# One issue order for every engine, read from a table: attention and two gated layers on one core

## The chip, the cores and the metric

The kernel runs on 1 core of one Trainium2 chip. The core has five engines with an instruction queue each: TensorE (PE in the profile, its weight loads PEld), VectorE (DVE), ScalarE (ACT), GpSimd (POOL) and SyncE (SP), which here issues every transfer. The metric is the device time of one execution in microseconds (us); less is better.

## The reference

A linear attention with 4 batches, 8 heads, 576 positions and a head width of 64 is followed by two gated layers over 2304 tokens (512 to 1536 to 512); all of it is float32.

```python
def phi(x):
    proj = np.einsum('bhsd,df->bhsf', x, w_phi)
    proj = proj - np.max(np.abs(proj), axis=-1, keepdims=True)
    return np.concatenate([np.exp(proj), np.exp(-proj)], axis=-1)
q_p, k_p = (phi(q), phi(k))
kv = np.einsum('bhsf,bhsd->bhfd', k_p, v)
z = np.sum(k_p, axis=2)
num = np.einsum('bhsf,bhfd->bhsd', q_p, kv)
den = np.einsum('bhsf,bhf->bhs', q_p, z)[..., None] + 1e-06
x = num / den
...
g = x @ w_gate
x = silu(g) * (x @ w_val) @ w_out
...
gate = 1.0 / (1.0 + np.exp(-(x @ w_gate)))
return gate * (x @ w_val) @ w_out
```

## The kernel before

**Attention** goes in 41 steps of 128 positions of 4 heads; the keys run 5 steps ahead of the queries. In a step, `proj` (L354) multiplies keys and queries by w_phi into one pair of PSUM banks, `a`, of which there is only one. `shift` on DVE takes the largest magnitude (L368, tile `m`) and subtracts it (L370, tile `sub`); only then may the next `proj` write `a`. `exps` on ACT (L377, tile `ek`) exponentiates the keys, `k_sum` (L397) adds them up against the values, `turn` (L419) transposes the queries, `turn_exp` on ACT (L430, tile `eq`) exponentiates these, and `ratio` (L447, bank `d`) makes numerators and denominators, which `ratio_out` (L453, tile `nd`) copies out on ACT. `den_load`, `den_inv` (L473 and L474 on DVE, tile `rc`) and `den_store` fetch denominators from DRAM, invert them and store them.

**Weights** arrive as float64 and are turned into float32 in 72 rounds (`plan_round`): `load` (tile `raw`), `mag` (L173) and `tail` (L176) on ACT, three `lead` operations on DVE (L181 to L187, tile `wcv`), `add` (L194) on POOL or DVE and mostly a `store` to DRAM. 18 rounds lie beside the attention. `plan_slot` and `plan_x_block` then form sums of quarters of weights and activations and split each into a high part (L223, on ACT) and a low part (L218, on DVE), so that a float32 product is three matmuls.

**The layers** (two of them, each in two halves of the width 1536) go over blocks of 512 or 256 tokens and pairs of width chunks. `product` (L664, banks `a` and `b`) makes seven products of quarters instead of eight; `keep` (L684) copies a bank to SBUF on ACT while later products go on adding into the same bank, `add` (L690) adds on DVE, `gate` (L702, ACT) and `gated` (L707, DVE) follow, their result is split (L714, L715) and `accumulate` (L736, L738, banks `c` and `d`) multiplies it by the output weights. For the first layer, `load_num` fetches numerators (tile `xraw`) and inverted denominators (tile `rb`), and `norm` (L584) multiplies them.

**The order.** Every step is registered with a time (`Plan.at`), worked out from a few constants (`STEP`, `RL`, `W2` and others), and the steps are traced in the order of these times. The framework's scheduler then puts the instructions of each engine in an order of its own, from a cost model: it may move an instruction ahead of an earlier one that it thinks is not ready, and it may part the instructions of one step. `issue_after` holds some copies and multiplications (in `mag`, `halves`, `norm`) behind the last instruction noted in `anchor`. On the chip each engine works through its own list in that order and waits at an instruction whose inputs are not there.

Of the kernel before, what the change touches and what calls it, by code (L numbers as in the profile page):

```python
# [2 lines left out]

# [6 lines left out]
F32 = mybir.dt.float32  # L10
# [79 lines left out]


class Plan:

# [17 lines left out]
def body(ctx: ExitStack, tc: tile.TileContext, qT, kT, v, w_phi2, wpk, out):  # L111
# [40 lines left out]

    anchor = {"early": True}
    stored = set()

    def plan_round(t, l, p, i, home=None):
# [62 lines left out]

    def halves(hi, lo, src, act):  # L220
        act = act or anchor["early"]
        with tc.issue_after(anchor["act" if act else "dve"].ins):
            (nc.scalar.copy if act else nc.vector.tensor_copy)(hi, src)  # L223
        low(hi, lo, src)

    def plan_slot(t, hh, p, gap=3.0, out=14.0):
# [30 lines left out]
        def split(w, m):  # L257
            if (hh, p) not in wts:
                wts[hh, p] = [pools[f"w{p}"].tile([P, 2, 2, 7, P], R32, tag=f"w{p}{x}",
                                                  name=f"w{p}{x}{hh}") for x in "hl"]  # L260
            d, src = ((slice(0, 4), a), (slice(4, 7), s))[m]
            halves(*(x[:, w, :, d] for x in wts[hh, p]), src[w], WA)

# [7 lines left out]
        def split_out():  # L271
            hi, lo = wts[hh, p, "o"]
            halves(hi, lo, lo.bitcast(F32), WA)

        def split_home():
            wts[hh, p, "o"] = [pools[f"w{p}"].tile([P, 2, DM], R32, tag=f"o{p}{x}",
                                                   name=f"o{p}{x}{hh}") for x in "hl"]
            halves(*wts[hh, p, "o"], a[2], WA)

        if not isinstance(t, float):  # L280
            for i, u in enumerate(t):
                e = plan_round(u, l, q, i, home)
                if i < 4 and i % 2:
                    at(e + 0.8, sums, i // 2)
                    for m in range(2):
                        at(e + 2.4 + 1.5 * m, split, i // 2, m)
                elif i == 5:
                    at(e + 1.0, split_home)
# [8 lines left out]
        at(t + out + 4.0, split_out)  # L297


    def plan_attention(ap, ak, ae, aq, t0):  # L300
# [4 lines left out]
        def consts():  # L305
            nc.sync.dma_start(out=w2, in_=w_phi2)
            make_identity(nc, ident)

        at(-99.0, consts)

        n = 2 * NT
# [45 lines left out]
        def shift(r, kinds):  # L357
# [6 lines left out]
            else:  # L364
# [4 lines left out]
                                    apply_absolute_value=True)  # L369
            anchor["dve"] = nc.vector.tensor_tensor(  # L370
                out=y, in0=x, in1=mm.to_broadcast(list(x.shape)), op=ALU.subtract)

        def exps(r):
            r["e"] = ak.tile([P, 4, 2, F], F32, tag="ek", name="ek", bufs=EB)
            e = r["e"].rearrange("p (c i) s f -> p i c s f", i=2)
            for s in range(2):
                anchor["act"] = nc.scalar.activation(e[:, :, :, s], r["sub"][:, :, 1], AF.Exp,  # L377
                                                     scale=-1.0 if s else 1.0)
# [44 lines left out]
        def turn_exp(i, c):  # L423

            qd, tt = divmod(i, NT)
            for g, lo, hi in here(tt):
                if (qd, g) not in eqt:
                    eqt[qd, g] = aq.tile([P, 4, 2, 320], F32, tag="eq", name="eq", bufs=EB)
                d = slice(lo - GROUPS[g][0], hi - GROUPS[g][0])
                anchor["act"] = nc.scalar.activation(  # L430
                    eqt[qd, g][:, :, c, d], qt[i]["pt"][:, :, lo - tt * P:hi - tt * P], AF.Exp,
                    scale=-1.0 if c else 1.0)
# [125 lines left out]
    def plan_x_block(t, hh, j, gap):  # L558
        n = BLOCKS[j][1]
        full = n == 2 * NQ  # L560
        t0 = BLOCKS[j][0]
        b, s, rb = {}, {}, {}

# [17 lines left out]
        def norm(c, k):  # L581
            x = b[c][:, k, :n]
            with tc.issue_after(anchor["dve"].ins):
                nc.vector.tensor_tensor(out=x, in0=x, in1=rb[c][:, k, :n], op=ALU.mult)  # L584

        def keep_x(c):

            if j not in ROUTE[1][:2]:
                nc.sync.dma_start(out=xo[0][j][:, c], in_=b[c][:, :, :n])
                stored.add(("x", 0, j, c))  # L590
            b[c] = b[c].rearrange("p k n -> p (k n)")[:, :2 * n] if full else b[c][:, :, :n]
            b[c] = b[c].rearrange("p (q n) -> p q n", n=NQ) if full else b[c]

# [6 lines left out]
        def sums(c):  # L600
# [4 lines left out]
            if full:  # L605
                b11, b12, b21, b22 = (b[c][:, k] for k in range(4))
                t3, t2, t4 = (s[c][:, k] for k in range(3))
# [4 lines left out]
                tt(out=t4, in0=b21, in1=t2, op=ALU.subtract)  # L612
                rb[c] = t1
            else:
                tt(out=s[c][:, 0], in0=b[c][:, 1], in1=b[c][:, 0], op=ALU.subtract)

        def split(c, m):
# [4 lines left out]
            if full:  # L622
                src, d = ((b[c][:, 0], 0), (rb[c], 1), (b[c][:, 2:4], slice(2, 4)),
                          (s[c][:, :2], slice(4, 6)), (s[c][:, 2], 6))[m]
            else:
                src, d = ((b[c], slice(0, 4, 2)), (s[c][:, 0], 4))[m]
            halves(*(x[:, c, d] for x in xs[hh, j]), src, XA)

# [8 lines left out]
        for c in range(2):  # L637
# [3 lines left out]
            for k in range(m):  # L641
                at(t + 5.0 + gap * (2 * c + 2 * k / m), split, c, k)

# [36 lines left out]
    def keep(r, k):  # L680


        src, d = {1: ("x", 0), 5: ("y", 3), 6: ("x", 1)}[k]
        anchor["act"] = nc.scalar.copy(part_of(r, d), parts(r, src))  # L684

    def add(r, d):


        c = part_of(r, d)
        anchor["dve"] = nc.vector.tensor_tensor(out=c, in0=parts(r, "zy x"[d]), in1=c, op=ALU.add)  # L690

# [17 lines left out]
    def gated_split(r, j, f):  # L709
        n = BLOCKS[j][1]  # L710
        v = r["c", f][:, 1].rearrange("p t n -> p (t n)")[:, :n]
        hi, lo = (pools["u"].tile([P, 2 * NQ], R32, tag=f"u{x}{f}", name=f"u{x}{f}")[:, :n]
                  for x in "hl")
        nc.scalar.copy(hi, v)  # L714
        nc.vector.tensor_tensor(out=lo, in0=v, in1=hi, op=ALU.subtract)  # L715
        r["u", f] = hi, lo

# [91 lines left out]
    def plan_unit(t, r, hh, j, p, last):  # L809
# [4 lines left out]
        for k in ORDER_LAST if (hh, j, p) == (3, len(BLOCKS) - 1, NPAIR - 1) else ORDER[full]:  # L814
# [14 lines left out]
            for d in ([3] if full and k == 7 else [2] if k == 4 else  # L829
# [3 lines left out]
                if d != 3:  # L833
                    at(e + 1.2, gated_split, r, j, d // 2)
        return t
# [19 lines left out]

    at(T0, lambda: anchor.update(early=False))
    T0 += TS
# [19 lines left out]
    SG, XG = 2.72, 2.13  # L877
    XA, WA, OA = True, True, 2

# [62 lines left out]
```

## Time and profile before

| | |
|---|---|
| median of 3 runs | 1056.11 us (1052.02 to 1059.38) |
| profiled execution | 1062.7 us, its span 1060.7 us, granted TensorE clock 0.994 |
| PE | 1021.9 us busy, 96% of the span; weight loads 905.9 us, 85% |
| DVE, ACT, POOL | 690.8, 534.5 and 24.0 us busy |
| chain that ended last, by engine | PE 61%, transfers 13%, DVE 10%, ACT 4% |

The span runs from the first to the last instruction of the program; 2.0 us of the execution lie around it. Busy times overlap, so they don't add up to the span. A matmul's recorded time is longer than the distance to the next matmul's start, since they are pipelined.

### The profile page before, as it was taken

The numbers are of one execution on the slowest core, as the hardware profiler recorded it, in microseconds if no ns is written. First come the engines' busy times: TensorE is split into PE (matmuls) and PEld (weight loads), VectorE is DVE, ScalarE is ACT, GpSimd is POOL, SyncE is SP. The second block draws the span as 40 slices with busy tenths as digits, with TensorE's granted clock in tenths as the row PEclk, the third lists the DMA queues.
The fourth block names the chain that finished last, engine by engine and source line by source line (L and its number), as shares of the span: only waits on it lengthen the run. The fifth ranks groups of instructions, "written<-read, shape, count | busy, mean of one in ns | idle before, by whom it ended". The sixth has DMA issues, their size and how long they took to land.

```text
span 1060.7 us, 20675 instructions
## 1 busy us (share of the span) xinstructions
PE 1021.9 (96%) x8488; PEld 905.9 (85%) x8488; DVE 690.8 (65%) x1246; ACT 534.5 (50%) x1029; POOL 24.0 (2%) x24
## 2 busy tenths in 40 slices
PE   6798999999999999999999999999999999999998
PEld 5565666688899899999899988999889999999997
DVE  4787775576785877546868698567586752463533
ACT  4667775654554555436445455455455542332422
POOL 0111110000000000000000000000000000000000
PEclk9899999999999999999999999999999999999999
DMA  5545655532664553106646444064344100331111
GB/s 184 160 151 169 201 179 155 176 104 95 194 214 131 169 169 100 40 24 206 189 142 207 137 153 159 20 206 165 127 140 159 60 21 18 122 120 40 41 40 40
DMA packets 67838, 135.99 MB, mean 128 GB/s; under 512 B 9696, under 2 KB 36000, under 8 KB 67744
## 3 DMA queue, kind: packets, MB, share of 16 engines
q1 hardware_dynamic: 67744, 134.68, 40.4%
q8 instruction: 66, 1.08, 0.4%
q14 instruction: 28, 0.23, 0.1%
HBM read 94.66 MB, written 39.99 MB: 127 GB/s over the span
## 4 chain that ended last, share of the span: by engine, by line
PE 61%; DMA 13%; DVE 10%; ACT 4%; issue 2%; SPq 1%; POOL 0%; DVEq 0%; ACTq 0%
PE a L664 20%; PE b L664 14%; DMA raw<-wpk 6%; PE c L738 6%; PE d L738 5%; PE d L736 4%; PE c L736 4%; PE d L447 3%; DMA xo<-o 2%; PE a L354 2%; DVE c L690 1%; DMA b<-xo 1%; PE c L397 1%; PE b L419 1%; DMA part<-o 1%
## 5 line engine op out<-in xcount | busy, mean ns | idle before, releaser
L702 ACT ACTIVATE c<-c 128x256 f32<-128x256 f32 x96 | 50.3, 524 | 146.8 <-DVE c L690 146.8
L684 ACT COPY c<-a 128x512 f32<-128x512 f32 x96 | 56.1, 585 | 103.0 <-PE a L664 92.6
L715 DVE TENSOR_TENSOR ul<-c,uh 128x512 fp32r<-128x512 f32 (+1 forms) x120 | 75.8, 636 | 46.7 <-ACT uh L714 46.3
L714 ACT CAST uh<-c 128x512 fp32r<-128x512 f32 (+1 forms) x120 | 68.8, 577 | 62.3 <-DVE c L707 57.1
L690 DVE TENSOR_TENSOR c<-b,c 128x512 f32<-128x512 f32 x96 | 65.7, 685 | 46.7 <-PE b L664 44.6
L664 PE MATMUL a<-xh,w1h 128*128 128x256 f32 x288 | 80.8, 280 | 2.0 <-DVE c L690 1.1
L664 PE MATMUL a<-xh,w2h 128*128 128x256 f32 x288 | 80.6, 280 | 1.8 <-ACT c L684 1.8
L664 PE MATMUL a<-xh,w0h 128*128 128x256 f32 x288 | 80.8, 281 | 1.5 <-DVE c L690 1.5
L181 DVE TENSOR_SCALAR wcv<-wcv 128x512 f32<-128x512 f32 x72 | 31.1, 431 | 78.4 <-ACT wcv L173 78.1
L664 PE MATMUL a<-xl,w0h 128*128 128x256 f32 x288 | 80.4, 279 | 0.0
L664 PE MATMUL a<-xl,w2h 128*128 128x256 f32 x288 | 80.4, 279 | 0.0
L664 PE MATMUL a<-xh,w0l 128*128 128x256 f32 x288 | 80.4, 279 | 0.0
L664 PE MATMUL a<-xh,w2l 128*128 128x256 f32 x288 | 80.4, 279 | 0.0
L664 PE MATMUL a<-xl,w1h 128*128 128x256 f32 x288 | 80.3, 279 | 0.0
L664 PE MATMUL a<-xh,w1l 128*128 128x256 f32 x288 | 80.3, 279 | 0.0
L176 ACT ACTIVATE raw<-raw 128x512 int32<-128x512 uint32 x72 | 48.7, 677 | 53.3 <-DMA raw<-wpk 52.6
L447 PE MATMUL d<-eq,z 128*32 128x320 f32 (+3 forms) x512 | 69.6, 422 | 4.9 <-ACT nd L453 3.0
L707 DVE TENSOR_TENSOR c<-c 128x256 f32<-128x256 f32 x96 | 53.3, 556 | 25.6 <-ACT c L702 25.2
L354 PEld LDWEIGHTS a<-w,x 64*128 64x128 f32 x576 | 39.0, 199 | 31.8 <-issue 19.6
L368 DVE TENSOR_REDUCE m<-a 128x8 f32<-128x1024 f32 (+1 forms) x41 | 44.7, 1091 | 31.1 <-PE a L354 30.7
L354 PE MATMUL a<-w,x 64*128 64x128 f32 x576 | 47.8, 301 | 17.5 <-DVE sub L370 9.6
L664 PE MATMUL b<-xh,w2h 128*128 128x256 f32 x224 | 62.5, 279 | 0.7 <-ACT c L684 0.7
(179 smaller groups left out, 3176.1 us busy)
## 6 DMA issues: line engine op xcount, KB each, us to landing
raw<-wpk SPq DMA_DIRECT2D x72, 512.0 KB
wf<-wcv SPq DMA_DIRECT2D x40, 256.0 KB
a<-wf SPq DMA_DIRECT2D x20, 512.0 KB
b<-xo SPq DMA_DIRECT2D x16, 512.0 KB
part<-o SPq DMA_DIRECT2D x13, 512.0 KB
o<-part SPq DMA_DIRECT2D x13, 512.0 KB
wfo<-wcv SPq DMA_DIRECT2D x20, 256.0 KB
v<-v SPq DMA_DIRECT2D x36, 132.0 KB
```

The costliest lines, as they stand in the source:

```text
L176: nc.scalar.activation(r["lo"].bitcast(I32), r["lo"], AF.Copy, scale=2.0 ** -29)
L354: nc.tensor.matmul(r["ps"][:, i, n, c], xt[kind, qd, j][d, c, o:o + P], w2[d], start=True, stop=True)
L447: nc.tensor.matmul(pn[i * w:(i + 1) * w, :m], f, e[:, h, c, :m], start=(c == 0), stop=(c == 1))
L664: nc.tensor.matmul(o, f[:, c], x[:, c], start=k == first and w == 0 and c == 0 and m == 0, stop=c == 1 and m == 2, skip_group_check=True)
L684: anchor["act"] = nc.scalar.copy(part_of(r, d), parts(r, src))
L690: anchor["dve"] = nc.vector.tensor_tensor(out=c, in0=parts(r, "zy x"[d]), in1=c, op=ALU.add)
L702: nc.scalar.activation(o, g, AF.Silu if hh < 2 else AF.Sigmoid)
L707: nc.vector.tensor_tensor(out=o, in0=v, in1=places(r, j, 0, d)[1], op=ALU.mult)
L714: nc.scalar.copy(hi, v)
L715: nc.vector.tensor_tensor(out=lo, in0=v, in1=hi, op=ALU.subtract)
L736: nc.tensor.matmul(ps[:, :n], a[:, k], x, start=st, stop=sp)
L738: nc.tensor.matmul(ps, x[:, k], a, start=st, stop=sp)
```

## The change

A table `TIMES` gives an issue time for each of the 3586 steps, in hundredths of a us, by the name of the step's function; `Plan.at` takes the next one of that name and leaves the time worked out from the constants unused. The steps are traced in the order of these times under `tc.manual_schedule()`, so that each engine's list is that order: no scheduler moves anything, and the instructions of one step stay together. `issue_after` and `anchor` go. So that the table can place the high and the low part of a split apart, `halves` becomes two steps, `high` and `rest`. Work, tiles, buffers and engines are the same, instruction by instruction.

```diff
+TIMES = {
...
+    "proj": (
...
 class Plan:
     def __init__(self):
         self.events = []
+        self.given = {name: iter(times) for name, times in TIMES.items()}
     def at(self, t, fn, *args):
+        if self.given:
+            t = next(self.given[fn.__name__])
         self.events.append((t, len(self.events), fn, args))
...
         def mag():
             r["w"] = scratch("wcv", U32)[:, :HW]
-            with tc.issue_after(anchor["act"].ins):
-                nc.scalar.activation(r["w"].bitcast(F32), r["hi"].bitcast(F32), AF.Abs)
+            nc.scalar.activation(r["w"].bitcast(F32), r["hi"].bitcast(F32), AF.Abs)
...
-    def halves(hi, lo, src, act):
-        act = act or anchor["early"]
-        with tc.issue_after(anchor["act" if act else "dve"].ins):
-            (nc.scalar.copy if act else nc.vector.tensor_copy)(hi, src)
-        low(hi, lo, src)
+    def plan_halves(t, views):
+
+        def high():
+            hi, _, src = views()
+            nc.scalar.copy(hi, src)
+
+        def rest():
+            low(*views())
+
+        at(t, high)
+        at(t + 0.6, rest)
...
-                at(t + 6.0 + gap * (2 * w + m), split, w, m)
+                plan_halves(t + 6.0 + gap * (2 * w + m), partial(split, w, m))
...
-    plan.issue()
+    with tc.manual_schedule():
+        plan.issue()
```

The order that comes of it, at three places. **Place A** is on ACT in the attention, around the step whose keys are exponentiated at 83.9 us of the profiled execution; `ek<-sub` is the exponential of the keys, `eq<-b` that of the queries, `nd<-d` the copy of a ratio, `w1h` the high part of a weight, and the rows that read `raw` are `mag` and `tail` of a round. Before:

```order
L377 ACTIVATE ek<-sub 128x2x2x128 x2
L173 ACTIVATE wcv<-raw 128x512
L176 ACTIVATE raw<-raw 128x512
L430 ACTIVATE eq<-b 128x4x128
L223 CAST w1h_1151<-a 128x2x512
L430 ACTIVATE eq<-b 128x4x128
L453 COPY nd<-d 128x256 x2
L377 ACTIVATE ek<-sub 128x2x2x128 x2
```

In the changed kernel, from the same exponential on:

```order
L722 ACTIVATE ek<-sub 128x2x2x128 x2
L798 COPY nd<-d 128x256
L562 CAST w1h_1130<-a 128x2x512
L775 ACTIVATE eq<-b 128x4x128 x2
L562 CAST w1h_1130<-s 128x2x384
L722 ACTIVATE ek<-sub 128x2x2x128 x2
L798 COPY nd<-d 128x256
L511 ACTIVATE wcv<-raw 128x512
```

The copy `nd<-d` moves ahead of the cast and of the queries, and the next row of the kind `raw<-raw` (L514) comes only nine rows after the last of these, behind two more exponentials of keys.

**Place B** is on DVE, near the end of the attention; `rc` is a tile of denominators that a transfer brings. Before:

```order
L368 TENSOR_REDUCE m<-a_2300 128x8
L473 TENSOR_SCALAR rc<-rc 128x18
L370 TENSOR_TENSOR sub<-a_2300,m 128x1024
L474 RECIPROCAL rc<-rc 128x18
L368 TENSOR_REDUCE m<-a_2361 128x4
L370 TENSOR_TENSOR sub<-a_2361,m 128x2x256
```

In the changed kernel, at the same step:

```order
L928 TENSOR_TENSOR xraw<-xraw,rb 128x512 x4
L713 TENSOR_REDUCE m<-a_2325 128x8
L715 TENSOR_TENSOR sub<-a_2325,m 128x1024
L556 TENSOR_TENSOR xl<-xraw,xh 128x256
L713 TENSOR_REDUCE m<-a_2387 128x4
L715 TENSOR_TENSOR sub<-a_2387,m 128x2x256
L556 TENSOR_TENSOR xl<-xraw,xh 128x256
L957 TENSOR_TENSOR t<-xraw 128x256
L958 TENSOR_TENSOR rb<-xraw 128x256
L959 TENSOR_TENSOR t<-xraw,rb 128x256
L960 TENSOR_TENSOR t<-xraw,t 128x256
L818 TENSOR_SCALAR rc<-rc 128x18
```

The denominators no longer part a reduction from its subtraction and come after two steps' worth of both; the four multiplications of `norm` for the first block, which stood behind this step, stand ahead of it.

**Place C** is on ACT in the first layer, in the fourth block of the route; `c<-a` and `c<-b` are `keep`, `xh` is the high part of the next block's activations. Before:

```order
L684 COPY c_4371<-b 128x2x256
L223 CAST xh<-xraw 128x256
L176 ACTIVATE raw<-raw 128x512
L173 ACTIVATE wcv<-raw 128x512
L223 CAST xh<-rb 128x256
L223 CAST xh<-xraw 128x512
L223 CAST xh<-t 128x512
L223 CAST xh<-t 128x256
L684 COPY c_4349<-a 128x2x256
```

In the changed kernel, from the same first row on:

```order
L1034 COPY c_4350<-b 128x2x256
L562 CAST xh<-t 128x256
L1034 COPY c_4321<-a 128x2x256
L562 CAST xh<-xraw 128x256
L514 ACTIVATE raw<-raw 128x512
L562 CAST xh<-xraw 128x512
L511 ACTIVATE wcv<-raw 128x512
L514 ACTIVATE raw<-raw 128x512
```

The `keep` of the unit's product 6 stood behind seven rows of preparation and now stands behind one.

## Rows read from the trace of the kernel before

**Rows 1.** The page's busy times: busy us, share of the span, instructions of each engine.

```profile
PE 1021.9 (96%) x8488; PEld 905.9 (85%) x8488; DVE 690.8 (65%) x1246; ACT 534.5 (50%) x1029; POOL 24.0 (2%) x24
```

**Rows 2.** Busy time by stretch (start:end in us, length, engines, clock, DMA share, GB/s).

```profile
20.90:67.20 46.30, 39.78 (x578) 28.80 (x578) 38.46 (x49) 31.78 (x63) 7.75 (x6) 0.93 0.51 149
67.20:139.50 72.30, 66.67 (x941) 44.14 (x940) 55.36 (x73) 51.78 (x105) 11.62 (x9) 0.98 0.61 185
139.50:175.70 36.20, 35.68 (x553) 25.15 (x552) 24.04 (x27) 23.88 (x52) 3.89 (x3) 1.00 0.64 176
175.70:201.80 26.10, 23.33 (x242) 14.14 (x242) 19.18 (x39) 16.05 (x39) 0.00 (x0) 0.93 0.46 147
201.80:1057.00 855.20, 843.45 (x6011) 782.79 (x6009) 545.82 (x1048) 402.63 (x762) 0.00 (x0) 1.00 0.37 118
```

**Rows 3.** The same stretches for L354 alone (`proj`): PE busy (x), PEld busy (x).

```profile
20.90:67.20 46.30, 11.38 (x144) 9.70 (x144) 0.93 0.51 149
67.20:139.50 72.30, 15.70 (x208) 12.94 (x208) 0.98 0.61 185
139.50:175.70 36.20, 9.56 (x128) 7.90 (x128) 1.00 0.64 176
```

**Rows 4.** Waits from 67.2 to 139.5 us: us in total, times, longest us.

```profile
ACT raw L176 <- DMA raw<-wpk: 10.1, 7, 2.6
DVE wcv L181 <- ACT wcv L173: 9.9, 7, 2.3
...
PE d L447 <- ACT nd L453: 3.0, 2, 1.8
```

**Rows 5.** Timeline from 83 us: start, length, instruction, [idle before <- releaser].

```profile
85.61 0.43 DVE L181 TENSOR_SCALAR wcv<-wcv 128x512 f32<-128x512 f32 x1 [2.11 <-ACT wcv L173]
...
87.60 0.68 ACT L176 ACTIVATE raw<-raw 128x512 int32<-128x512 uint32 x1 [2.02 <-DMA raw<-wpk]
...
90.08 0.64 ACT L453 COPY nd<-d 128x256 f32<-128x256 f32 x2
...
90.50 0.62 PE L447 MATMUL d<-eq,z 128*32 128x256 f32 x2 [1.75 <-ACT nd L453]
```

**Rows 6.** Timeline of DVE from 175 us.

```profile
176.98 1.23 DVE L368 TENSOR_REDUCE m<-a 128x8 f32<-128x1024 f32 x1 [1.64 <-PE a L354]
181.18 0.18 DVE L473 TENSOR_SCALAR rc<-rc 128x18 f32<-128x18 f32 x1 [2.97 <-DMA rc<-den]
181.27 1.22 DVE L370 TENSOR_TENSOR sub<-a,m 128x1024 f32<-128x1024 f32 x1
```

**Rows 7.** Timeline of PE in the same stretch.

```profile
182.63 0.71 PE L354 MATMUL a<-w,x 64*128 64x128 f32 x8 [2.30 <-DVE sub L370]
```

**Rows 8.** Timeline of ACT from 352 us.

```profile
361.07 0.41 ACT L223 CAST xh<-xraw 128x256 fp32r<-128x256 f32 x1 [2.05 <-DVE xraw L584]
361.51 0.68 ACT L176 ACTIVATE raw<-raw 128x512 int32<-128x512 uint32 x1
...
364.29 0.59 ACT L684 COPY c<-a 128x512 f32<-128x512 f32 x1
```

**Rows 9.** Timeline of PE in the same stretch.

```profile
364.93 0.38 PE L664 MATMUL a<-xh,w2h 128*128 128x256 f32 x1 [1.80 <-ACT c L684]
```

**Rows 10.** Timeline of DVE from 205 us.

```profile
211.99 0.42 DVE L252 TENSOR_TENSOR s<-a 128x256 f32<-128x256 f32 x1 [8.97 <-DMA a<-wf]
```

**Rows 11.** Transfers of `raw` in the chain that ended last: start, us, what.

```profile
99.61 3.81 DMA raw<-wpk
...
740.70 7.46 DMA raw<-wpk
```

**Rows 12.** Busy time by stretches of 10 us, columns as in the second group.

```profile
40.00:50.00 10.00, 5.90 (x80) 5.10 (x80) 8.07 (x10) 6.02 (x14) 2.58 (x2) 0.70 0.55 150
```

**Rows 13.** Waits in the whole span.

```profile
ACT raw L176 <- DMA raw<-wpk: 52.6, 34, 4.3
...
ACT wcv L173 <- DMA raw<-wpk: 14.2, 8, 2.8
```

More of the change, by code (lines that the diff above doesn't have):

```diff
@@ L2 @@
 from contextlib import ExitStack
+from functools import partial
 import concourse.bass as bass
@@ L89 @@
           for o, n in (((0, 256), (256, 320)) if b % 2 == 0 else ((0, 320), (320, 256)))]
+TIMES = {
+    "consts": (
+        118,),
+    "make_identity": (
+        75,),
+    "load": (
[12 rows of a table added]
+    "load_v": (
+        162, 249, 336, 423, 1041, 1331, 1625, 1844, 2274, 2544, 2918, 3502, 3876, 4272, 4923,
+        5297, 5807, 6449, 6719, 7196, 7590, 8068, 8361, 8806, 9309, 9579, 10402, 10568, 11116,
+        11510, 11987, 12281, 12725, 13228, 13498, 14378,),
+    "proj": (
[3 rows of a table added]
+    "shift": (
[3 rows of a table added]
+    "exps": (
+        701, 949, 1285, 1574, 1829, 2236, 2628, 3068, 3586, 3982, 4452, 5007, 5381, 5891, 6285,
+        6833, 7226, 7674, 8048, 8422, 8890, 9286, 9719, 10245, 10547, 11119, 11594, 11968, 12342,
+        12809, 13187, 13582, 14164, 14463, 15186, 15600,),
+    "k_sum": (
[3 rows of a table added]
+    "kv_keep": (
+        2091, 2119, 3876, 3904, 6205, 6232, 8164, 8192, 10190, 10217, 12083, 12111, 14109, 14137,
+        15862, 15889,),
+    "turn": (
[3 rows of a table added]
+    "turn_exp": (
[6 rows of a table added]
+    "ratio": (
[4 rows of a table added]
+    "ratio_out": (
[4 rows of a table added]
+    "ratio_store": (
[4 rows of a table added]
+    "den_load": (
+        5174, 7519, 9622, 11237, 13542, 15467, 17359, 18109,),
+    "den_inv": (
+        5578, 8037, 10138, 11956, 13801, 16003, 20439, 18651,),
+    "den_store": (
+        5851, 8111, 10187, 12031, 13905, 16052, 20488, 18700,),
+    "part_banks": (
+        17045,),
+    "swap": (
+        17221, 17861,),
+    "product": (
[60 rows of a table added]
+    "keep": (
[12 rows of a table added]
+    "add": (
[17 rows of a table added]
+    "gate": (
[13 rows of a table added]
+    "gated": (
[13 rows of a table added]
+    "high": (
[25 rows of a table added]
+    "rest": (
[25 rows of a table added]
+    "accumulate": (
[19 rows of a table added]
+    "out_sum": (
[3 rows of a table added]
+    "out_store": (
[3 rows of a table added]
+    "out_load": (
+        45941, 46168, 49631, 50050, 53694, 54213, 57665, 58295, 84938, 85358, 88593, 89504, 91346,
+        91554, 92366,),
+    "mag": (
[6 rows of a table added]
+    "tail": (
[6 rows of a table added]
+    "lead": (
[17 rows of a table added]
+    "sums": (
[5 rows of a table added]
+    "store": (
[5 rows of a table added]
+    "load_num": (
+        14256, 14421, 16917, 18185, 23116, 23712, 25369, 25893, 30205, 31930,),
+    "norm": (
+        15107, 15168, 15228, 15289, 17662, 17972, 18960, 19145, 23544, 23578, 24154, 24188, 26056,
+        26117, 26638, 26775, 30781, 30842, 32506, 32672,),
+    "keep_x": (
+        15243, 15424, 18044, 19217, 23623, 24276, 25099, 25525, 29191, 29617,),
+    "load_out": (
+        17316, 36145, 37654, 39162, 56718, 58227, 59736, 77293, 78802, 80311,),
+}
 class Plan:
@@ L261, in split @@
             d, src = ((slice(0, 4), a), (slice(4, 7), s))[m]
[L262 removed]
+            return *(x[:, w, :, d] for x in wts[hh, p]), src[w]
         def load_out():
@@ L582, in norm @@
             x = b[c][:, k, :n]
-            with tc.issue_after(anchor["dve"].ins):
-                nc.vector.tensor_tensor(out=x, in0=x, in1=rb[c][:, k, :n], op=ALU.mult)
+            nc.vector.tensor_tensor(out=x, in0=x, in1=rb[c][:, k, :n], op=ALU.mult)
         def keep_x(c):
@@ L590, in keep_x, with quarters @@
                 stored.add(("x", 0, j, c))
-            b[c] = b[c].rearrange("p k n -> p (k n)")[:, :2 * n] if full else b[c][:, :, :n]
-            b[c] = b[c].rearrange("p (q n) -> p q n", n=NQ) if full else b[c]
+        def quarters(c):
+            if hh:
+                return b[c]
+            x = b[c].rearrange("p k n -> p (k n)")[:, :2 * n] if full else b[c][:, :, :n]
+            return x.rearrange("p (q n) -> p q n", n=NQ) if full else x
         def load(c):
@@ L683, in keep @@
         src, d = {1: ("x", 0), 5: ("y", 3), 6: ("x", 1)}[k]
-        anchor["act"] = nc.scalar.copy(part_of(r, d), parts(r, src))
+        nc.scalar.copy(part_of(r, d), parts(r, src))
     def add(r, d):
         c = part_of(r, d)
-        anchor["dve"] = nc.vector.tensor_tensor(out=c, in0=parts(r, "zy x"[d]), in1=c, op=ALU.add)
+        nc.vector.tensor_tensor(out=c, in0=parts(r, "zy x"[d]), in1=c, op=ALU.add)
     def places(r, j, w, d):
@@ L711, in gated_split @@
         v = r["c", f][:, 1].rearrange("p t n -> p (t n)")[:, :n]
[L712 to L716, printed above, removed]
+        if ("u", f) not in r:
+            r["u", f] = [pools["u"].tile([P, 2 * NQ], R32, tag=f"u{x}{f}", name=f"u{x}{f}")[:, :n]
+                         for x in "hl"]
+        return *r["u", f], v
     acc, outs = {}, {}
```

49 lines of the change are left out of this document (25 added, 24 removed), and 271 rows, old and new, of the table TIMES.

## The prediction

> **What bounds the kernel now.** I read the page's busy times first: PE is busy for 96% of the span, DVE for 65%, ACT for 50% [rows 1]. The span less PE's busy time is 1060.7 - 1021.9 = 38.8 us. No instruction is removed, so an order can give back idle time and little else. Next the stretches [rows 2], to see where that idle time lies: from 201.8 us on, in the layers, PE idles 855.2 - 843.45 = 11.75 us; in the 180.9 us of attention between 20.9 and 201.8 it idles 15.4 us (6.5, 5.6, 0.5, 2.8), with its heaviest DVE load, 83% and 77%, in the first two stretches.
>
> For the attention, busy time says too little, so I count steps. A step issues 16 matmuls of `proj`, so the third group gives 9, 13 and 8 steps in three stretches [rows 3], and their lengths [rows 2] give 46.3/9 = 5.14, 72.3/13 = 5.56 and 36.2/8 = 4.53 us for a step. The work differs less: 578/9 = 64, 941/13 = 72 and 553/8 = 69 matmuls a step. At the pace of the third stretch the second would take 13 x 4.53 x 72.4/69.1 = 61.7 us, 10.6 less than it does, and the first 9 x 4.53 x 64.2/69.1 = 37.9, 8.4 less. So PE's recorded 92% in the second stretch hides lost time twice as long as its 5.6 us of idling.
>
> The Trainium skill, Perfetto Trace Analysis, section Identifying the Most-Contended Engine, says the same of the measure: the matmul row's occupancy tells little of how far TensorE is from its roofline, and the share of weight loads is to be used. By occupancy these two stretches could give at most 12.2 us, by pace 19.0; the weight loads' 61% in the second stretch against 69% in the third agree with the pace, as the trace's step counts do.
>
> What makes a step long is seen in the waits of the second stretch [rows 4]: ACT waits 10.1 us in 7 places for a `raw` transfer, and DVE 9.9 us in 7 places for the `mag` of ACT. One instance is place A [rows 5]: `lead` makes DVE wait 2.11 us with the next reduction behind it; ACT stands 2.02 us at `tail` for its transfer; `nd<-d`, queued behind, comes at 90.08, and PE, whose bank `d` it frees, has waited 1.75 us. These are waits in a queue for work that nobody needs at once.
>
> **The change part by part.** *Attention, rounds and ratios.* At place A the new list has `nd<-d` right behind the exponential and `tail` far behind, so the 2.02 us falls on nothing urgent, and PE's 1.75 us with it, if the transfer has landed by then: `raw` transfers in the chain take from 3.81 to 7.46 us [rows 11], two steps or less. What is late next is DVE. Its work stays, 38.46 us in the first stretch and 55.36 in the second [rows 2], so these can't fall to 37.9 and 61.7 us without DVE at 101% and 90%. DVE's chain from `proj` to subtraction leaves it waiting at times, so I take a share of about 91% and 86% for what is reached: 46.3 to 42.3 and 72.3 to 64.3 us, 4 and 8 us. Ends: 0 and 0 if DVE's queue only trades one wait for another, 6 (DVE at 95%) and 10.6 at best. The nearest row is the third stretch, which runs at its pace with the last rounds (3 additions on POOL) in it and PE idle for 0.5 us.
>
> *Attention, denominators.* At place B, `rc` waits 2.97 us for a transfer between a reduction and its subtraction [rows 6], and the next `proj` starts 2.30 us late for it [rows 7]. With `rc` behind two more pairs this goes: 2.3 to 3.0 us, I take 3 since the copies behind it slide too. What could replace it are the four `norm` rows ahead of the reduction: 0.68 us each if their data is there, and a new wait if not. The table places their transfers two steps ahead of them, so I add nothing, with up to 4 us (a transfer of 3.81 [rows 11]) as the bad end.
>
> *The clock.* In the stretch from 40 to 50 us the granted clock is 0.70 on average, after PE was busy for only 5.90 of these 10 us [rows 12]: of two levels, 6 us were at 1.2 GHz instead of 2.4, worth up to 3 us. That lies inside the first stretch and is in its pace, so it isn't counted again.
>
> *The layers.* Place C is typical: `keep`, on which PE's next product waits, stands behind a split that itself waits 2.05 us, then behind `tail`, `mag` and four splits [rows 8]; PE loses 1.80 us [rows 9]. At 211.99 DVE has stood 8.97 us at a sum of weights for its transfer, with an `add` behind [rows 10]. The new order puts `keep` second, and on SP the transfer of that sum goes ahead of five stores of ratios that it stood behind. Products and accumulations keep their order but for a few places, and ACT at 402.63 and DVE at 545.82 of 855.2 us [rows 2] have room to do preparation between urgent rows. Of 11.75 us I take 8: two thirds, because new lists have late transfers of their own. Ends: 11.75, and -6 (half as much idling again) on the bad side.
>
> *Other edits.* `issue_after` gone, and a split in two steps, cost nothing by themselves: they issue no instruction, and only the lists above decide. SP's transfers move too; a store that waits holds later loads, which is part of the bad ends.
>
> Sum: 4 + 8 + 3 + 8 = 23 us of the profiled execution's 1062.7, so 1039.7. The median is 1056.11/1062.7 = 0.9938 of that execution, so **1033 us**.
>
> **The rivals.** *DVE binds the attention.* For it: 83% of the first stretch, with the `proj` chain on the same queue [rows 2]. Against it: waits of 9.9 us for `mag` in that queue are idle time [rows 4]. Then 4 + 8 becomes some 3, the sum 14, the time 0.9938 x 1048.7 = 1042.
>
> *The order hardly differs from what the engines lived by.* The scheduler had also sorted by a model. For it: the third stretch is already dense [rows 2]. Against it: three places that the trace shows waiting are changed. Then within 10 us of 1056, say 1052.
>
> *Slower: late transfers on ACT in the layers.* 54 rounds lie beside the layers. ACT waits for `raw` 42 times, 66.8 us in all, at either operation [rows 13], 1.6 us each. If the new list puts `mag` and `tail` only a landing time behind each load, each of 54 may wait that long again, 86 us of ACT with `keep` queued behind. In place C 2.05 us of waiting made 1.80 us of PE idling. If half of 86 us passes on to PE, 43 less the 11.75 it has now is +31; with 10 us won in the attention, 1056 + 21 = 1077. It decides from the point where `keep` is later than PE's other products last: at place C a delay of 3.22 us, from 361.07 to 364.29 [rows 8], was enough. Against it: the chain's shorter transfers are 3.81 us, and place C moves such rows behind `keep`.
>
> **How the numbers follow.** Chances: the forecast 0.66, DVE binding 0.16, no difference 0.10, late transfers 0.08. The low end is the whole 38.8 us of PE idling: 0.9938 x 1023.9 = 1018. The high end takes half of the attention's sum and nothing in the layers: 1062.7 - 7.5 = 1055.2, times 0.9938 = 1049, which takes in the rival of DVE. What is left out is about 0.18. A change of 1% (1045.5) is about what a measurement of this kernel can tell from none. Faster by more than that: 0.66 and two thirds of 0.16, with a little of the forecast's own spread taken off, 0.76; within 1%: 0.15; slower: 0.09.
>
> **What would show it right or wrong.** Right: the first product starts near 187 us instead of 201.8; steps in the loaded part of the attention near 4.9 us; no DVE wait at `rc` between a reduction and its subtraction; PE idling of about 4 us in the layers. Wrong: long waits of DVE for `mag` or of ACT for `raw` as before, `norm` waiting for `rb` ahead of a reduction, or PE waits behind `keep` in more places than now. A lower granted clock anywhere in the layers would break the sum, since every matmul there is priced at full clock.

## The result and the profile after

The changed kernel takes 1024.74 us (median of 4 runs, 1022.55 to 1027.88) against 1054.64 (4 runs, 1052.02 to 1059.38): a ratio of 0.9714, 95% interval 0.9668 to 0.976. Its profiled execution took 1027.88 us with a span of 1026.1, 34.6 less than before. The first product starts at 180.9 us instead of 201.8, so 20.9 us come from the attention, and from there to the end it takes 845.2 us instead of 858.9, 13.7 less. The two medians differ by 29.9 us, the two profiled executions by more: the one before, of 1062.7 us, lies 8.1 above its median, the one after 3.1. What is read from the traces below adds up to the 34.6 us.

The page's busy times and its chain that ended last, of the changed kernel; the first line answers to [rows 1]:

```profile
PE 996.8 (97%) x8488; PEld 896.6 (87%) x8488; DVE 708.0 (69%) x1246; ACT 535.7 (52%) x1029; POOL 24.7 (2%) x24
...
PE 87%; DVE 6%; DMA 2%; ACT 1%; issue 1%; SPq 0%; DVEq 0%
```

PE's recorded idle time fell by only 9.5 us (38.8 to 29.3), its recorded busy time by 25.1, with the same 8488 matmuls. So most of what was gained had stood in the record as busy PE.

Busy time by stretch, cut at the starts of projections that stand near those of [rows 2], and the first three stretches for the projection's line alone, as in [rows 3]:

```profile
22.70:60.00 37.30, 31.94 (x514) 23.59 (x514) 31.94 (x39) 28.73 (x56) 5.24 (x4) 1.00 0.51 153
60.00:121.80 61.80, 59.26 (x984) 43.52 (x984) 54.72 (x68) 50.41 (x102) 9.75 (x7) 1.00 0.65 192
121.80:155.90 34.10, 32.06 (x510) 22.87 (x508) 26.25 (x34) 25.89 (x54) 6.47 (x5) 1.00 0.75 217
155.90:180.90 25.00, 21.79 (x238) 13.41 (x236) 20.34 (x39) 17.23 (x41) 0.00 (x0) 0.93 0.56 175
180.90:1022.50 841.60, 837.25 (x6002) 780.81 (x6000) 560.51 (x1046) 400.83 (x759) 0.00 (x0) 1.00 0.36 119
```

```profile
22.70:60.00 37.30, 9.31 (x130) 7.93 (x130) 1.00 0.51 153
60.00:121.80 61.80, 16.25 (x224) 13.74 (x224) 1.00 0.65 192
121.80:155.90 34.10, 8.13 (x112) 6.91 (x112) 1.00 0.75 217
```

By projections (16 a step) the loaded part has 14 steps in 61.80 us, 4.41 each where it had 5.56, and the stretch before it 8.1 steps of 4.59 where it had 5.14. The third stretch went the other way: 7 steps of 4.87 us, with 73 matmuls a step, where it had 4.53 with 69. DVE is at 89% and 86% in the loaded part and the stretch before it; that is close to a limit, but in the loaded part DVE still waits 5.1 us for PE to fill bank `a`, so DVE alone doesn't set the pace.

Place A now, on ACT (start, length, instruction); it answers to [rows 5]:

```profile
85.92 0.41 ACT L798 COPY nd<-d 128x320 f32<-128x320 f32 x1
86.22 0.69 ACT L514 ACTIVATE raw<-raw 128x512 int32<-128x512 uint32 x1
86.80 0.68 ACT L511 ACTIVATE wcv<-raw 128x512 f32<-128x512 f32 x1
```

The copy out of bank `d` goes ahead of `tail` and `mag`, and neither of these waits. Of the waits in [rows 13] this is left from 181 us on; ahead of the first product ACT no longer waits for `raw` at all:

```profile
ACT raw L514 <- DMA raw<-wpk: 4.9, 5, 3.1
...
ACT wcv L511 <- DMA raw<-wpk: 3.2, 3, 1.9
```

Place B, on DVE and then on PE, answers to [rows 6] and [rows 7]:

```profile
157.76 1.29 DVE L928 TENSOR_TENSOR xraw<-xraw,rb 128x512 f32<-128x512 f32 x2 [1.38 <-DMA rb<-rden]
158.97 1.22 DVE L713 TENSOR_REDUCE m<-a 128x8 f32<-128x1024 f32 x1
...
165.98 0.17 DVE L818 TENSOR_SCALAR rc<-rc 128x18 f32<-128x18 f32 x1
```

```profile
161.67 1.02 PE L699 MATMUL a<-w,x 64*128 64x128 f32 x8 [1.91 <-DVE sub L715]
```

`rc` comes late enough not to wait, but two `norm` rows in front of a reduction now wait 1.38 us for their transfer. PE's next projection stands 1.91 us for it, and then the granted clock falls to its lower level, 1.2 GHz:

```profile
158.00:162.00 4.00, 2.09 (x47) 1.39 (x44) 3.75 (x5) 2.40 (x6) 0.00 (x0) 0.99 1.03 389
162.00:165.00 3.00, 3.00 (x36) 2.44 (x34) 2.24 (x5) 1.93 (x5) 0.00 (x0) 0.50 0.04 12
```

In the layers PE waits 3 times, 3.9 us in all, where it had 14 waits of 11.3 us. Three of the eight kinds of wait before, and then all that are left:

```profile
PE a L664 <- DVE c L690: 2.7, 2, 1.5
PE a L664 <- ACT c L684: 2.6, 2, 1.8
PE c L736 <- DVE ul L715: 2.2, 5, 0.9
```

```profile
PE c L1085 <- ACT uh L562: 1.5, 1, 1.5
PE a L1014 <- DVE c L1040: 1.4, 1, 1.4
PE c L1085 <- DVE ul L556: 1.0, 1, 1.0
```

### The profile page after: what moved, and what is told of

Its sections match the earlier page's. It is cut to its first block, busy times and chain, and to the rows that moved or that the text cites. A ratio compares the mean times of both kernels' runs of the same rounds, so it can differ in the third digit from the quotient of the medians.

```text
span 1026.1 us, 20688 instructions
## 1 busy us (share of the span) xinstructions
PE 996.8 (97%) x8488; PEld 896.6 (87%) x8488; DVE 708.0 (69%) x1246; ACT 535.7 (52%) x1029; POOL 24.7 (2%) x24
## 4 chain that ended last, share of the span: by engine, by line
PE 87%; DVE 6%; DMA 2%; ACT 1%; issue 1%; SPq 0%; DVEq 0%
PE a L1014 28%; PE b L1014 21%; PE c L1087 8%; PE c L1085 7%; PE d L1085 7%; PE d L1087 6%; PE d L792 4%; PE a L699 3%; PE c L742 3%; PE b L764 2%; DVE sub L715 1%; DVE m L713 1%; DMA rb<-rden 1%; DVE wcv L525 1%; DVE ul L556 1%
## 5 line engine op out<-in xcount | busy, mean ns | idle before, releaser
L1052 ACT ACTIVATE c<-c 128x256 f32<-128x256 f32 (+1 forms) x96 | 50.2, 524 | 176.4 <-DVE c L1040 176.1
L1052 ACT ACTIVATE c<-a 128x256 f32<-128x256 f32 x60 | 23.0, 384 | 81.5 <-PE a L1014 81.3
L1057 DVE TENSOR_TENSOR c<-c 128x256 f32<-128x256 f32 (+1 forms) x96 | 52.9, 554 | 16.5 <-ACT c L1052 15.8
L699 PE MATMUL a<-w,x 64*128 64x128 f32 x576 | 45.0, 293 | 19.3 <-DVE sub L715 7.5
L1014 PE MATMUL b<-xh,w0l 128*128 128x256 f32 x224 | 62.4, 278 | 0.0
L1014 PE MATMUL b<-xh,w1l 128*128 128x256 f32 x224 | 62.3, 278 | 0.0
L1014 PE MATMUL b<-xh,w0h 128*128 128x256 f32 x224 | 62.3, 278 | 0.0
L1014 PE MATMUL b<-xl,w0h 128*128 128x256 f32 x224 | 62.3, 278 | 0.0
```

The lines of the kernel that those rows point to most:

```text
L699: nc.tensor.matmul(r["ps"][:, i, n, c], xt[kind, qd, j][d, c, o:o + P], w2[d], start=True, stop=True)
L1014: nc.tensor.matmul(o, f[:, c], x[:, c], start=k == first and w == 0 and c == 0 and m == 0, stop=c == 1 and m == 2, skip_group_check=True)
L1052: nc.scalar.activation(o, g, AF.Silu if hh < 2 else AF.Sigmoid)
L1057: nc.vector.tensor_tensor(out=o, in0=v, in1=places(r, j, 0, d)[1], op=ALU.mult)
```

## The experiments

In this table "first" is the start of the first product and "rest" the span from there; "gaps" are the times from one matmul's start to the next one's in the rest, where they are over 0.26 us, by number and sum (the longest regular spacing is 0.23; at half the clock an accumulation takes 0.43 and is counted too); "low" is the time at 1.2 GHz ahead of the first product, and behind it up to the last matmul, summed from the granted clock in windows of 1 us. All times are us, each of one profiled execution, but for the medians; the ratio is to the kernel before on the same chip.

| kernel | median | ratio, 95% interval | first | rest | gaps | low |
|---|---|---|---|---|---|---|
| before | 1054.64 | | 201.8 | 858.9 | 36, 24.3 | 13.6 / 0 |
| after | 1024.74 | 0.9714 (0.9668 to 0.976) | 180.9 | 845.2 | 16, 10.5 | 3.4 / 3.4 |
| before_order | 1072.46 | 1.0168 (1.0123 to 1.0213) | 196.8 | 870.8 | 65, 44.1 | 17.0 / 17.1 |
| attn_before | 1043.37 | 0.9896 (0.9852 to 0.9939) | 203.2 | 840.4 | 17, 10.3 | 26.5 / 4.2 |
| layers_before | 1051.45 | 0.9984 (0.9951 to 1.0017) | 179.0 | 866.9 | 66, 43.1 | 3.4 / 10.2 |
| table_sched | 1066.07 | 1.0118 (1.008 to 1.0156) | 204.8 | 857.9 | 42, 28.8 | 27.3 / 3.4 |
| rounds_before | 1046.55 | 0.9918 (0.9883 to 0.9952) | 202.5 | 846.7 | 15, 10.8 | 13.7 / 3.4 |
| proj_before | 1036.09 | 0.9845 (0.9798 to 0.9892) | 195.4 | 838.3 | 13, 8.5 | 19.0 / 1.5 |
| unit_before | 1044.64 | 0.9917 (0.9884 to 0.995) | 183.6 | 861.4 | 34, 23.4 | 10.3 / 3.4 |
| prep_before | 1052.52 | 0.9988 (0.9966 to 1.0009) | 181.1 | 869.5 | 57, 42.2 | 6.8 / 17.1 |
| tail_early | 1036.74 | 0.9845 (0.9807 to 0.9882) | 189.7 | 840.4 | 10, 5.7 | 13.6 / 0 |
| tails_layers | 1038.29 | 0.9856 (0.9818 to 0.9893) | 184.0 | 854.1 | 35, 23.7 | 10.2 / 6.8 |
| fewer_waits | 1020.40 | 0.9700 (0.9666 to 0.9735) | 177.8 | 839.7 | 11, 5.0 | 0 / 0 |
| fewer_waits2 | 1020.32 | 0.9687 (0.9654 to 0.9719) | 178.6 | 840.5 | 9, 4.1 | 3.4 / 0 |

How much two executions differ without a difference of order can be read from this table. In attn_before, rounds_before, proj_before and tail_early the engines go through the layers in the changed kernel's order, and the rest of these five lies between 838.3 and 846.7 us. In layers_before, unit_before, prep_before and tails_layers they go through the attention in its order, and the first product of these five starts between 179.0 and 184.0; before_order and attn_before share the old order there, and start at 196.8 and 203.2. So a difference of less than some 8 us in "rest", or 6 in "first", in one execution isn't by itself one of the order. The medians are from several chips, on which the median of the kernel before was 1051.8 to 1054.6; the ratios are free of that.

All runs but one keep the changed kernel's code and alter numbers of its table. The theory was the prediction's: where the table puts the steps makes the gain, by taking rows that wait for transfers out of the way of rows that PE waits for.

**The order of the kernel before, whole or in part.** Every step gets the place at which the trace of the kernel before shows it starting (before_order), or only the steps that started ahead of the first product there (attn_before), or behind it (layers_before). The places are counted from the neighbouring projections and products, most of which keep the table's own numbers. A step stays whole, and 22 of 3586 had to move by over 0.5 us for a buffer or an operand (5 and 20 in the two halves). Of some 230, 120 and 200 altered lines one, of the first two runs:

```diff
     "tail": (
-        1121, 1513, 1690, 2533, 2743, 5123, 5569, 6540, 6708, 8570, 8809, 10818, 10874, 12546,
+        1090, 1216, 1460, 2528, 3435, 4101, 4652, 5629, 6205, 6972, 7489, 8285, 8694, 9407,
```

> Same code as the changed kernel, but the numbers of the table are the start times that the trace of the kernel before shows for each step, so every engine gets the order in which the kernel before ran, with each step whole. Theory (where the table puts the steps makes the gain): back near the kernel before, 1048 to 1058 us, first product at 197 to 203 us, PE idle 9 to 13 us from there on. Rival (a fixed order with whole steps and without the scheduler makes the gain, whatever its numbers): 1025 to 1033 us, first product near 181.

> Only the steps that the kernel before started ahead of its first product (the attention and what lies beside it) get its order back; the layers keep the table's. Theory: the 20.9 us of the attention are lost again, 1042 to 1047 us, first product at 197 to 203 us, the rest of the span within 3 us of the 845.2 of the changed kernel. Rival (the gain is one of the fixed order): 1025 to 1030.

> Only the steps that the kernel before started after its first product get its order back; the attention keeps the table's. Theory: first product near 181 us as in the changed kernel, PE idle 9 to 13 us from there on against 4.35, 1033 to 1039 us. Rival (the 13.7 us of the layers are not the order of preparation but come from the matmuls' own pace): PE idle 9 to 13 us but under 5 us of time lost, 1025 to 1029.

before_order lost all of the gain and more, 1072.46 us: a fixed order with whole steps gives nothing by itself. The halves lose 18.6 us (attn_before) and 26.7 (layers_before), together 45.3 of the 47.7 that the whole loses, so the two parts of the gain add up, as far as these medians can tell. attn_before came out as the theory had it, but for a rest 4.8 us shorter than the changed kernel's, which is within the spread above. layers_before lost more than it should have: its rest is 8 us longer than in the kernel before itself, and that of before_order 12. The scheduler had moved single instructions of a step among those of others, and a step kept whole can't follow that; that this is what costs is not shown. In the attention nothing can be said of whole steps: of the two starts, 196.8 and 203.2 us, one is earlier and one later than in the kernel before.

**The numbers with the scheduler.** The one run that alters code:

```diff
-    with tc.manual_schedule():
-        plan.issue()
+    plan.issue()
```

> The table's numbers stay, but the framework's scheduler sorts the steps' instructions again. Theory (positions count, and the scheduler moves rows that wait for nobody ahead of urgent ones): part of the gain is lost, 1030 to 1050 us. Rival (the numbers as a program order suffice): 1022 to 1029, as the changed kernel.

1066.07 us, with the first product at 204.8 and a rest of 857.9: at neither place is anything left of the gain. Both theory and rival fell short here; I had expected a part of it to stay. The chain that ended last in that run, against 87% PE in the changed kernel:

```profile
PE 64%; DVE 13%; DMA 12%; ACT 4%; issue 2%; SPq 1%; POOL 0%; DVEq 0%; ACTq 0%; POOLq 0%
```

So the change is worth its 30 us only as a pair: the table's places and nobody who moves them. The order of the old constants without the scheduler was not tried.

**Which steps, in the attention.** The preparation's 189 steps at the places of the kernel before (rounds_before), or the attention's own 509 (proj_before). One line of each:

```diff
     "den_inv": (
-        5578, 8037, 10138, 11956, 13801, 16003, 20439, 18651,),
+        5752, 7880, 9558, 11430, 13722, 15536, 17486, 18651,),
```

(this one of proj_before; in rounds_before the line of `tail` shown above reads nearly the same).

> In the attention only the preparation of weights (rounds, sums, splits, the first block's normalisation and their transfers; 189 steps) gets the places it had in the kernel before, counted from the neighbouring projections; projections, exponentials, transposes, ratios and denominators stay where the table has them. Theory of the prediction (rows that wait for transfers stood in front of urgent ones): most of the attention's 21 us is lost again, first product at 193 to 200 us, 1036 to 1043 us, ACT waiting over 10 us for raw transfers ahead of the first product. Rival (the attention's own steps were in a bad order among themselves): first product by 186 us, 1024 to 1031 us.

> The complement: in the attention the 509 steps of the attention itself (projections, subtractions, exponentials, transposes, ratios, denominators and their transfers) get the order of the kernel before, the preparation of weights stays where the table has it. Theory: first product by 187 us, 1025 to 1032 us. Rival: first product at 193 to 203 us, 1036 to 1045 us.

rounds_before lost the attention's whole gain, 21.6 us, with time and first product above the theory's ranges, and ACT waits for `raw` again (waits up to 202.5 us):

```profile
ACT raw L514 <- DMA raw<-wpk: 20.5, 12, 3.4
```

But proj_before lost 14.5 us too, where the theory allowed 6: that is the rival's range. Ahead of its first product the record has no wait of ACT for `raw` and none of DVE for `mag`. What came back there is the wait at `rc`, 5.2 us against 1.5 in the changed kernel, and 15.6 us more at 1.2 GHz:

```profile
DVE rc L818 <- DMA rc<-den: 5.2, 2, 2.9
```

So the waits for `raw` aren't the whole of the attention's gain. The two losses add up to more than that gain; that either half alone meets the other in the wrong place, since the places of preparation were laid around the projections' order, is how I read it, and not shown.

**One suspected wait by itself.** 18 numbers put each `tail` of the attention close behind its load:

```diff
     "tail": (
-        1121, 1513, 1690, 2533, 2743, 5123, 5569, 6540, 6708, 8570, 8809, 10818, 10874, 12546,
+        1033.9, 822.6, 834, 1948.6, 2229.3, 3681.8, 3839.1, 5709.6, 6148.7, 6964.2, 7358.7, 9180.1, 9139.3, 10331.4,
```

> The changed kernel with 18 numbers altered: the tail of each attention round, which needs only its raw transfer, goes 2.8 to 5.7 us behind the load's place, as in the kernel before, instead of 5 to 20 us; everything else keeps its place. This takes the suspected wait by itself: rows of ACT that wait for a transfer in front of urgent rows. Theory: ACT waits 15 to 35 us for raw ahead of the first product against 4.9, the first product starts at 184 to 192 us, 1028 to 1036 us. Rival (ACT has room enough, and the loss in the kernel before came from DVE's rows and from the order of the rest): ACT waits as long, but the first product is within 2 us of 180.9, 1022 to 1028 us.

The waits of ACT ahead of the first product at 189.7 us:

```profile
ACT raw L514 <- DMA raw<-wpk: 13.5, 11, 3.8
```

No such wait stood there in the changed kernel; in the kernel before it was this:

```profile
ACT raw L176 <- DMA raw<-wpk: 14.9, 11, 2.6
```

So nearly all of ACT's old waiting is back, and 8.8 of the 20.9 us with it: 13.5 us of waiting cost 0.65 us for each, or 0.4 to 0.8 against first products of 179.0 to 184.0. Of the 8.8, up to 5.1 is the clock: 10.2 us more at 1.2 GHz, half of which is lost if PE is what binds there. The waiting was a little under what I had expected, the first product within the theory's range, the median 0.7 us above it.

The same in the layers, with 54 tails 2.8 us behind their loads:

```diff
-        12728, 12956, 13818, 13874, 20085, 20613, 20670, 24449, 24947, 25114, 25250, 26992, 27159,
+        12728, 12956, 13818, 13874, 19736, 19779, 20048, 24160, 24513, 24600, 25018, 26802, 26862,
```

> The changed kernel with 54 numbers altered: the tail of each round beside the layers goes 2.8 us behind the place of its load (4.1 to 11.1 us before), so that nearly every one has to wait for its transfer on ACT. It is the price of the prediction's third rival (late transfers on ACT in the layers) put to the test. If half of each such wait passes on to PE: ACT waits 70 to 110 us for raw in the layers, 35 to 55 us are lost, 1058 to 1080 us. If ACT, busy for half of the time there, takes most of it up: the same waits of ACT, under 15 us lost, 1024 to 1040 us, PE idle under 20 us from the first product on against 7.95.

The waits from 181 us on:

```profile
ACT raw L514 <- DMA raw<-wpk: 44.7, 26, 4.2
```

That is less waiting than I had expected, but 39.8 us more than in the changed kernel, and the rest is 8.9 us longer, 0.22 for each, or 0.2 to 0.4 against rests of 838.3 to 846.7. The other 3.1 of the span are the attention's, whose order was not touched: there the clock was low for 10.2 us instead of 3.4. So less than the half of such a wait that the prediction's third rival took reaches PE in the layers.

**Which steps, in the layers.** The units' own 1954 steps at the old places (unit_before), or the 927 of preparation (prep_before). Of each one line, `keep` in the first and `tail` in the second:

```diff
-        23533, 23939, 24899, 25036, 25448, 29150, 29287, 29561, 30449, 30520, 30932, 31896, 32081,
+        23601, 23939, 25074, 25191, 25448, 29206, 29307, 29560, 30429, 30540, 30932, 32066, 32253,
```

```diff
-        44560, 45345, 45912, 46125, 47957, 48906, 49908, 50058, 51079, 51213, 52016, 53315, 53430,
+        44278, 45196, 45604, 45942, 47579, 48434, 48897, 48973, 49604, 51125, 51791, 52710, 52941,
```

> In the layers the 1954 steps of the units themselves (products, keep, sums of products, gates, gated splits, accumulations, outputs) get the order of the kernel before; preparation stays where the table has it. Theory (preparation in front of urgent rows is what costs): within 4 us of the changed kernel, 1023 to 1029 us, PE idle under 10 us from the first product on against 7.95 counted the same way. Rival (the units' own order makes the gain): 1035 to 1050 us.

> In the layers only the 927 steps of preparation (rounds, sums, splits, blocks of x, their transfers) get the places of the kernel before; the units' own steps stay where the table has them. Theory: most of what the run with the whole order of the layers lost comes back, 1038 to 1050 us, PE idle 15 to 23 us from the first product on. Rival: under 1032 us.

prep_before lost all that layers_before did (rest 869.5 us); its median is 2.5 us above the theory's range. unit_before lost 16.2 us of the rest where the theory allowed 4, though its `keep` moved by 0.3 us in the median; its time is in the rival's range. 5 of these 16.2 are a slower pace of the matmuls (last section); the gaps rose by 12.9. As in the attention, neither half is the gain by itself.

**Fewer waits.** 13 numbers at the three places where the changed kernel's trace shows PE standing (`norm` at place B, `norm` at 271 us, a sum of weights at 566 us); two of the lines:

```diff
-        15107, 15168, 15228, 15289, 17662, 17972, 18960, 19145, 23544, 23578, 24154, 24188, 26056,
-        26117, 26638, 26775, 30781, 30842, 32506, 32672,),
+        15107, 15168, 15355, 15360, 17662, 17972, 18960, 19145, 23544, 23578, 24154, 24188, 26390,
+        26392, 26638, 26775, 30781, 30842, 32506, 32672,),
```

> The changed kernel with 13 numbers altered at three places where its trace shows PE standing: two norm rows behind the next subtraction instead of ahead of it (PE idle 1.91 us at 159.76 and half the clock from 161.9 to 165.3), two norm rows and their sums behind the gated values that the accumulations wait for (PE late by 3.4 us at 271.5 to 275 and half the clock to 277.9), a sum of weights behind two sums of products (1.5 us at 566.5). Theory: these waits are on the path and nothing is late in their place, 8 to 10 us gained, 1014 to 1019 us. Rival (the rows that are put off are late themselves, or the next transfer is): 1022 to 1028 us.

The two stretches shown above for place B, and PE's waits behind the first product, in this run:

```profile
158.00:162.00 4.00, 3.27 (x53) 2.15 (x54) 3.96 (x7) 3.68 (x10) 0.00 (x0) 1.00 0.85 326
162.00:165.00 3.00, 2.53 (x35) 1.61 (x30) 2.79 (x9) 2.44 (x9) 0.00 (x0) 1.00 0.15 42
```

```profile
PE c L1085 <- ACT uh L562: 0.6, 1, 0.6
PE c L1085 <- DVE ul L556: 0.3, 1, 0.3
```

The waits are gone or shorter, the clock doesn't fall before the last matmul in this execution, and its span is 1017.5, 8.6 less (3.1 in the attention, 5.5 behind it). The median, 1020.40, is 4.3 under that of the changed kernel, 1.4 above the range expected. But the kernel before was itself 2.9 faster on this chip, and the intervals of the two ratios, 0.9666 to 0.9735 and 0.9668 to 0.976, overlap. The rest is within the spread of one order, and the first product 1.2 us ahead of it: tail_early, whose layers were not touched, has a rest of 840.4, gaps of only 5.7 and no low clock there. So the trace shows the waits gone at these places; that they had cost time is not shown.

With four more rows put behind a subtraction in the attention:

```diff
-        5457, 5502, 5518, 6274, 6320, 6335, 6791, 6837, 6853, 7323, 8411, 8427, 8487, 8533, 8548,
+        5457, 5502, 5518, 6274, 6320, 6335, 6791, 6837, 6853, 7323, 8411, 8427, 8487, 8643, 8647,
```

> As the run before, and at two places of the attention the last two lead rows of a round go behind the next subtraction, with the sum of weights that needs them: there a lead row of DVE took 1.40 us instead of 0.43 while GpSimd's addition ran, and PE stood 1.94 us at 34.83 and 1.75 us at 89.21. Theory: 1 to 3 us less than the run before, these two PE gaps under 0.9 us, no lead row over 0.5 us at these places. Rival (the subtraction was late for another reason): gaps and time as in the run before.

The same time, 1020.32 us. The slow `lead` rows are gone (last section), and so is PE's pause of 1.75 us at 89.2. One of 1.35 us stands at 94.8 in its place, the pause at 34.8 is now one of 1.03 us at 35.9, and the first product is no earlier. That expectation of 1 to 3 us was wrong: the next thing was late by as much.

## Why the prediction was right

1033.0 us was forecast, 1018 to 1049 as the range; the time fell into it, 8 us under the forecast, because the attention's and the layers' terms were both too small. The path it named, waits in a queue for work that nobody needs at once, is borne out in part.

- *An order can give back idle time and little else.* This step failed. The time fell by 34.6 us and recorded idle time by 9.5. For the attention the prediction left this measure itself and went by pace. For the layers, and for the low end of the range, it kept to idle time. That the time came out above the low end, 1018 us, is therefore no support for it. The rule of the Trainium skill (Perfetto Trace Analysis, Identifying the Most-Contended Engine) that the prediction cited, that occupancy of the matmul row tells little, is borne out by these 34.6 and 9.5 us.
- *Attention, rounds and ratios, 4 + 8 us.* The mechanism is shown for a part: place A waits no more, and tail_early gives 8.8 us of the gain back by ACT's waits for `raw` alone. rounds_before gives back all of it, but proj_before gives back 14.5 us without any such wait, for which the prediction has no term but that of `rc`. The size was too small. I held the pace of the third stretch, 4.53 us a step, for the best case; the loaded steps now take 4.41, against 4.95 in the forecast. The DVE shares taken (91% and 86%) came out at 86% and 89%.
- *The clock.* I left it inside the first stretch. In the two profiled executions it was 13.6 us at 1.2 GHz ahead of the first product and is 3.4: up to 5.1 us of the 20.9. By all executions it doesn't show as a part of the gain: the granted clock is 0.996 on average in the 4 of the changed kernel (0.992 to 1.000) and in the 52 of the kernel before that were timed beside the experiments (0.991 to 0.998). In attn_before and table_sched, with 26.5 and 27.3 us of low clock ahead of the first product, the granted clock is lower in every execution (0.979 to 0.989). The sign of failure that the prediction named, a lower clock in the layers, came too, for 3.4 us at 274.6; at most 1.7 us were lost by it.
- *Denominators, 3 us.* The wait at `rc` went, and the bad end named beside it came in part: `norm` waits 1.38 us, PE 1.91. The last stretch is 25.0 us against 26.1, so 1.1 of the 3 was gained in these two executions. Undoing place B alone was not tried.
- *Layers, 8 us of 11.75 of idle time.* Idle time in the stretch fell from 11.75 to 4.35, 7.4 us: this term was right by its own measure. The rest fell by 13.7, because the record counts only a part of a gap as idle: gaps fell from 36 to 16 and from 24.3 to 10.5 us, and less a regular spacing of some 0.2 us for each of the 20 that is 9.8 us. A somewhat better pace of the matmuls makes 2.5 (116.02 to 115.48 ns, some 4700 times); 1.4 stays unassigned. The pace differs between executions of one order (last section), so these 2.5 aren't shown to be the table's.
- *The rivals.* DVE at 89% didn't keep the attention from gaining 20.9 us. The order did differ. Late transfers on ACT in the layers have a price of 0.2 to 0.4 for each us waited, so that even 86 us of them would have cost 17 to 34 and not 43, by estimate from tails_layers.

Left open is what makes up the rest of the attention's gain beside ACT's waits for `raw`, and why the kernel before's own interleaving of instructions is 18 us faster than the same order in whole steps (before_order); the few displaced steps and the interleaving weren't tried apart.

## What to carry to other kernels

Count a stretch's loss by steps and by start-to-start gaps of matmuls, not by PE's idle time: here a quarter of the gain was recorded idle. In an in-order queue a row that waits for a transfer costs by what stands behind it: here 0.4 to 0.8 us for each waited one where every step hangs on that engine, 0.2 to 0.4 where the engine is half idle. Place it behind its load by at least the time that the transfer takes to land. Before reading a few us out of one trace, compare executions that share an order: here they differed by up to 8. And treat an order as one piece: either half of it beside the other half of an old order lost most of the gain, and a scheduler on top of it lost all.

## What the runs showed of the hardware

**Matmuls have two paces at the full clock.** The same 576 products in a row, with the accumulations between them, take 108.08 us in the changed kernel and 105.64 in attn_before, PE busy throughout:

```profile
807.50:915.58 108.08, 108.08 (x752) 100.52 (x751) 54.25 (x97) 41.54 (x80) 0.00 (x0) 1.00 0.19 66
```

```profile
827.83:933.47 105.64, 105.64 (x753) 98.54 (x751) 53.97 (x97) 41.55 (x80) 0.00 (x0) 1.00 0.19 65
```

The products of 256 columns start 117.8 ns apart in the first and 114.2 on average in the second. A pace lasts for tens to hundreds of us. The Trainium skill (TensorE: Matmul & The Clock Gate, Wait — 56ns, not 53.3ns?) gives the columns at 2.4 GHz and some 2.5 ns more, 109.2 by estimate for 256 columns. Both measured paces are above it. Over all the profiled executions the mean lies between 114.4 and 116.6 ns, up to 10 us of a span. What sets the pace is open.

**A pause of PE can be paid twice.** Where PE stood 1.91 us at 159.76, the clock was at 1.2 GHz from 161.9 to 165.3; in fewer_waits, without the pause, it stayed at 2.4. Not every pause does this: behind the first product the kernel before has 36 gaps of 24.3 us and no time at 1.2 GHz.

**DVE and GpSimd.** One `lead` row took 1.41 us instead of 0.42 while GpSimd's addition ran; reductions and subtractions that read PSUM didn't change. The changed kernel on DVE and on GpSimd:

```profile
85.80 0.42 DVE L519 TENSOR_SCALAR wcv<-wcv 128x512 f32<-128x512 f32 x1
86.25 1.41 DVE L522 TENSOR_SCALAR wcv<-wcv 128x512 uint32<-128x512 uint32 x1
...
88.31 1.22 DVE L713 TENSOR_REDUCE m<-a 128x8 f32<-128x1024 f32 x1
```

```profile
86.02 1.36 POOL L532 TENSOR_TENSOR a<-wcv,raw 128x512 int32<-128x512 int32 x1 [14.46 <-ACT ek L722]
```

In fewer_waits2 the reduction stands beside the addition, and the `lead` row behind it is short:

```profile
86.46 1.22 DVE L713 TENSOR_REDUCE m<-a 128x8 f32<-128x1024 f32 x1 [0.29 <-PE a L699]
...
88.93 0.42 DVE L522 TENSOR_SCALAR wcv<-wcv 128x512 uint32<-128x512 uint32 x1
```

The Trainium skill (SBUF — State Buffer, SBUF: two separate sides) says that the two engines share one pair of ports under an exclusive lock. The trace agrees: the `lead` row takes 1.41 us and ends 0.28 us after the addition does.
